# Lightning attention and snake MLP on one core: q in pieces of four tokens, freely placed PSUM banks, whole-row stores and a new instruction order

## The chip, the cores and the metric

The kernel runs on one core of a Trainium2 chip. The metric is the device time of one launch in microseconds (us). The kernel before takes 216.03 us, the median of 13 runs (214.77 to 218.7).

## What is computed

For each of 4 batches and 8 heads, a causal linear attention with decay runs over 768 tokens of 64 elements. Its output, 3072 tokens by 512, goes through an MLP (512 to 2048 to 512) with the "snake" activation.

```python
# attention, in blocks of 64 tokens, for each batch and head
intra = ((q_b @ k_b.T) * lam ** (i - j) for j <= i) @ v_b
inter = (q_b * lam ** (i + 1)) @ state
out_b = intra + inter
state = lam ** 64 * state + (k_b * lam ** (63 - j)).T @ v_b
# MLP on x = out as [3072, 512]
h = x @ w_in
g = h + sin(alpha * h) ** 2 / alpha
result = g @ w_out
```

## The kernel before

**Tiling.** The 3072 tokens are cut into 6 groups g of 512 tokens (256 tokens of each of two batches). A group has 4 attention units u (one batch, 4 heads, 256 tokens), so there are 24 units; units 8 and up add to the state that the unit 8 places before left. The MLP of a group is 16 first-layer tiles f1 (each 4 matmuls of 128x128 by 512 columns) and 4 output tiles m, each in 4 chunks f2.g.m.j of 4 such matmuls.

**Names in the order.** A unit runs through: `ld` (load of q, k, v, 256 KB each, SP queue, L259), `sq` and `sk` (scaling by powers of lam to bf16, L300), `cv` (cast of v), `tq`, `tk` (four TensorE transposes into PSUM, units 0 to 7, L327) with `tcq`, `tck` (copies back to SBUF), or `tdq`, `tdk` (transposing DMAs on SP, units 8 to 23, L345), `s` (16 score matmuls, L368), `m` (mask multiply on VectorE, two halves, L378), `k` (k times v, L400), `kc` (its copies), `a` (the new state, L425), `n` (the decayed state), `oi` (state times q, L446), `o` (masked scores times v, L460), and `x` (copy of the result to the MLP's input tile xt). The MLP has `f1` (`f1a` is the half of a tile that needs only a group's first two units), `sin` and `sqr` on the activations, `stt` (the final multiply-add on VectorE, L516), `f2` (L525), `oc` (copy of an output tile) and `st` (its store, L540). `lt` and `ltc` are the last tile, cut in three. `w.N` stands for N matmuls of zeros.

**What sets the order.** One string, ORDER, lists every step with its engine (V VectorE, A ScalarE, G GpSimd, T TensorE, S SyncE) and, for PSUM tiles, the bank. Each engine runs its steps in that order. Semaphores hold a step back until its data is there and its buffer or bank is free. So a late step holds back everything behind it on its engine.

**PSUM.** There are 8 banks, numbered 0 to 7. Before the change the two score halves always take banks 4 and 5 and the two outputs of a unit banks 6 and 7; transposes, k times v, f1 and f2 take the bank given in ORDER.

**Loads and stores.** A load puts token pairs on a partition: 128 partitions by 4 heads by 512 B. An output tile of 128 tokens is stored as two DMAs of 64 partitions by 2 KB, since even and odd tokens lie in different partition halves. Loads from unit 4 on are held until f1.0.12 has run. w_in and w_out come in four parts each on GpSimd's queue; the last part of w_out (`wo.3`) is issued by GpSimd after `a.0.1`.

**Tables.** GpSimd raises lam to the powers of the position in one instruction (L220); VectorE makes from it the table E for q and its reciprocal R for k, copies both to PSUM (`tab`), and then scales unit 0.

Of the kernel before, what the change touches and what calls it, by code (L numbers as in the profile page):

```python
# [9 lines left out]
ALU = mybir.AluOpType  # L10
# [8 lines left out]
tab:V ld.0.0:S sq.0:V ap:T w.4:T:h0 tq.0:T:0 ld.0.1:S ld.0.2:S sk.0:V cv.0:A w.3:T:h1 tk.0:T:5 al:V  # L19
tck.0:V ld.1.0:S ld.1.1:S ld.1.2:S ld.2.0:S ld.2.1:S ld.2.2:S ld.3.0:S tcq.0:A k.0:T:1,2 a.0.0:V  # L20
w.4:T:oa s.0:T sq.1:G sk.1:G sq.2:G kc.0.0:A kc.0.1:V m.0.0:V w.3:T:oa tq.1:T:2 w.3:T:oa tk.1:T:4
cv.1:A tcq.1:A k.1:T:0,1 oi.0:T m.0.1:V o.0:T x.0.0:A x.0.1:A tck.1:V kc.1.0:V kc.1.1:A a.1.0:V
s.1:T sk.2:V cv.2:A w.5:T:h2 tq.2:T:6 tk.2:T:1 w.2:T:h2 k.2:T:2,0 ld.3.1:S m.1.0:V m.1.1:V kc.2.0:V
kc.2.1:V wi.0:G wi.1:G a.2.0:V sq.3:G sk.3:G n.2.0:G wi.2:G n.0.0:G tcq.2:A w.1:T:ob oi.1:T tck.2:A
ld.3.2:S o.1:T x.1.0:A x.1.1:A cv.3:A s.2:T tq.3:T:1 w.4:T:oa oi.2:T tk.3:T:0 w.2:T:h2 k.3:T:2,3
m.2.0:V m.2.1:V o.2:T tck.3:V wi.3:G wo.0:G wo.1:G tcq.3:A s.3:T x.2.0:A a.3.0:V kc.3.0:V m.3.0:V
x.2.1:A m.3.1:V w.6:T:h1 oi.3:T f1a.0.0:T:0 f1a.0.1:T:4 o.3:T x.3.0:A kc.3.1:V f1a.0.2:T:3
f1a.0.3:T:2 wo.2:G x.3.1:V f1.0.0:T f1.0.1:T sin.0.0:A sin.0.1:A f1.0.2:T sqr.0.0:V stt.0.0:V
sqr.0.1:G stt.0.1:V f1.0.3:T f1.0.4:T:5 f1.0.5:T:7 sin.0.2:A sin.0.3:A sqr.0.2:A stt.0.2:V sqr.0.3:A
sin.0.4:A sqr.0.4:V sin.0.5:A f1.0.6:T:1 stt.0.3:V sin.0.6:A sqr.0.5:G f1.0.7:T:6 stt.0.4:V  # L30
f1.0.8:T:0 sqr.0.6:V stt.0.5:V stt.0.6:V f1.0.9:T:2 f1.0.10:T:4 f1.0.11:T:3 sin.0.7:A sin.0.8:A
sqr.0.7:G stt.0.7:V sqr.0.8:A stt.0.8:V n.1.0:G sin.0.9:A sqr.0.9:V a.1.1:G stt.0.9:V sin.0.10:A
sqr.0.10:G sin.0.11:A sqr.0.11:V f1.0.12:T:1 sin.0.12:A sqr.0.12:A a.0.1:G wo.3:G a.2.1:G n.2.1:G
stt.0.10:V stt.0.11:V f1.0.13:T:5 f1.0.14:T:7 sin.0.13:A sin.0.14:A n.0.1:G n.1.1:G n.3.0:G ld.4.0:S
ld.4.1:S ld.4.2:S ld.5.0:S ld.5.1:S ld.5.2:S ld.6.0:S sqr.0.13:V stt.0.12:V stt.0.13:V sqr.0.14:A
stt.0.14:V ld.6.1:S ld.6.2:S ld.7.0:S ld.7.1:S ld.7.2:S ld.8.0:S ld.8.1:S f2.0.0.0:T:0 f1.0.15:T:2
f2.0.0.1:T f2.0.1.0:T:6 sq.4:G f2.0.3.0:T:3 sin.0.15:A sqr.0.15:V f2.0.2.0:T:1 f2.0.1.1:T f2.0.2.1:T
stt.0.15:V f2.0.2.2:T f2.0.0.2:T f2.0.0.3:T f2.0.3.1:T oc.0.0:V a.3.1:G sk.4:G tq.4:T:7 tk.4:T:2
ld.8.2:S ld.9.0:S ld.9.1:S ld.9.2:S tck.4:V tcq.4:A f2.0.1.2:T s.4:T ld.10.0:S cv.4:A sq.5:G
tq.5:T:0 sk.5:G sq.6:G tcq.5:A f2.0.1.3:T oc.0.1:A sk.6:G tk.5:T:2 cv.5:G m.4.0:V f2.0.3.2:T m.4.1:V  # L40
k.4:T:6,7 a.4.0:V tck.5:A s.5:T m.5.0:V tq.6:T:0 cv.6:A tcq.6:V kc.4.0:A tk.6:T:2 m.5.1:V kc.4.1:A
ld.10.1:S ld.10.2:S f2.0.2.3:T tck.6:A oi.4:T k.5:T:0,2 o.4:T oc.0.2:A x.4.0:A x.4.1:A sq.7:G sk.7:G
s.6:T a.5.0:V kc.5.0:A kc.5.1:A f2.0.3.3:T tq.7:T:1 m.6.0:V m.6.1:V tcq.7:V cv.7:G n.3.1:G oi.5:T
oc.0.3:A sq.8:G tk.7:T:4 n.4.0:G sk.8:G tck.7:V a.4.1:G o.5:T k.6:T:0,2 k.7:T:1,3 x.5.0:A x.5.1:A
s.7:T n.5.0:G tdq.8:S a.6.0:V w.2:T:oa oi.6:T kc.6.0:A o.6:T a.7.0:V f1a.1.0:T:0 x.6.0:A m.7.0:V
n.4.1:G ld.11.0:S tdk.8:S ld.11.1:S x.6.1:A kc.6.1:V f1a.1.1:T:2 cv.8:A kc.7.0:A m.7.1:V oi.7:T
o.7:T k.8:T:4,5 f1a.1.2:T:1 x.7.0:V x.7.1:A f1.1.0:T f1.1.1:T f1.1.2:T kc.8.0:A sq.9:G f1a.1.3:T:4
f1.1.3:T kc.7.1:A f1.1.4:T:7 sin.1.0:A sin.1.1:A sin.1.2:A sk.9:G ld.11.2:S sqr.1.0:V stt.1.0:V
sin.1.3:A cv.9:A sqr.1.1:G stt.1.1:V sq.10:G sin.1.4:A sqr.1.2:V sqr.1.3:A stt.1.2:V stt.1.3:V
kc.8.1:V f1.1.5:T:3 sin.1.5:A f1.1.6:T:0 sqr.1.4:G sqr.1.5:G f1.1.7:T:6 f1.1.8:T:1 k.9:T:4,5  # L50
sin.1.6:A stt.1.4:V stt.1.5:V sin.1.7:A f1.1.9:T:2 kc.9.0:V sqr.1.6:A f1.1.10:T:7 kc.9.1:A sqr.1.7:A
tdq.9:S s.8:T a.8.0:G sk.10:G st.0.0.0:S ld.12.0:S tdk.9:S st.0.0.1:S stt.1.6:V stt.1.7:V sin.1.8:A
sqr.1.8:A sin.1.9:A sin.1.10:A stt.1.8:V m.8.0:V f1.1.11:T:3 f1.1.12:T:0 f1.1.13:T:1 sq.11:G
tdq.10:S sin.1.11:A f1.1.14:T:4 ld.12.1:S ld.12.2:S ld.13.0:S sqr.1.9:V sqr.1.10:A sqr.1.11:G
# [76 lines left out]
def kernel(  # L131
# [123 lines left out]
    def load(u, j, **_):  # L255
# [7 lines left out]
        if (u, j) == (4, 0):  # L263
            after(loads[u, j], f1mm[HOLD])
# [361 lines left out]
```

## Time and profile before

| what | value |
|---|---|
| median of 13 runs | 216.03 us |
| the profiled execution's own time | 216.56 us |
| its span, first to last instruction | 213.7 us |
| TensorE (PE) busy | 203.8 us, 95% |
| VectorE (DVE), ScalarE (ACT), GpSimd (POOL) busy | 129.9, 123.4, 141.5 us |
| mean granted TensorE clock | 0.998 |
| bytes moved by DMA | 33.92 MB in 64009 packets |

The page gives busy time by engine, the span in 40 slices, the chain of work that ended last, the costliest groups, and the DMA issues. PE's busy time is modelled, so the timeline's starts of successive groups tell more than the sums. A few matmul records are missing: where a group of 4n matmuls shows one fewer, the gap of about 0.16 us ahead of it is the missing record.

### The profile page before, as it was taken

How to read it: one execution, taken by the hardware profiler on the slowest of the kernel's cores; microseconds unless marked ns; L12 is line 12 of the kernel's file. 1: busy time of each engine (PE TensorE's matmuls, PEld its weight loads, DVE VectorE, ACT ScalarE, POOL GpSimd, SP SyncE). 2: the span in 40 equal slices, each digit the busy share in tenths (PEclk: the TensorE clock that was granted, in tenths of full speed). 3: DMA queues.
4: the chain of work that ended last, by engine and by line, in shares of the span. 5: the costliest groups of instructions: out<-in, count | busy, mean ns of one | idle time of the engine just before them, and what ended most of it. 6: DMA issues, size and time to landing. Idle time of an engine off the chain costs nothing.

```text
span 213.7 us, 5465 instructions
## 1 busy us (share of the span) xinstructions
PE 203.8 (95%) x2104; PEld 109.8 (51%) x2132; DVE 129.9 (61%) x235; ACT 123.4 (58%) x244; POOL 141.5 (66%) x208
## 2 busy tenths in 40 slices
PE   7989999899999979999999999999999999999993
PEld 6668544357744544455545554454454444444463
DVE  3885797159599843678768685726884625432120
ACT  3463983067899828997485496936635659131001
POOL 5498389689697997999999986709841728030000
PEclk9999999999999999999999999999999999999999
DMA  5999999999977999957997879620610000162624
GB/s 132 298 223 185 202 207 278 281 291 289 196 162 195 220 248 217 311 117 167 228 290 131 214 134 243 116 49 0 135 41 3 0 0 0 36 154 59 149 49 98
DMA packets 64009, 33.92 MB, mean 159 GB/s; under 512 B 19680, under 2 KB 61040, under 8 KB 63984
## 3 DMA queue, kind: packets, MB, share of 16 engines
q1 hardware_dynamic: 59568, 29.31, 60.3%
q0 software_dynamic: 4224, 4.19, 12.2%
q8 instruction: 16, 0.26, 0.6%
q10 hardware_dynamic: 192, 0.07, 0.2%
q14 instruction: 9, 0.07, 0.1%
HBM read 27.28 MB, written 6.29 MB: 157 GB/s over the span
## 4 chain that ended last, share of the span: by engine, by line
PE 72%; DMA 9%; POOL 5%; ACT 5%; issue 4%; SPq 2%; DVE 1%; POOLq 0%; ACTq 0%
PE ops L525 31%; PE hps L482 29%; DMA w_out_sb<-in_moe_w_out_dram 4%; ACT s L502 4%; PE okv L460 3%; DMA st_q<-in_q_dram 3%; DMA QT<-KD 2%; PE sp L368 2%; PE okv L446 2%; PE ops L550 2%; SPq L259 2%; POOL s L511 1%; PE kvp L400 1%; POOL QL L300 1%; POOL KD L300 1%
## 5 line engine op out<-in xcount | busy, mean ns | idle before, releaser
L482 PE MATMUL hps<-xt,w_in_sb 128*128 128x512 bf16 (+1 forms) x404 | 86.4, 363 | 0.6 <-issue 0.2
L525 PE MATMUL ops<-w_out_sb,gall 128*128 128x512 bf16 x352 | 83.2, 379 | 2.4 <-issue 1.3
L516 DVE SCALAR_TENSOR_TENSOR gall<-s,r_sb,hps 128x512 bf16<-128x512 bf16 x96 | 68.3, 743 | 23.8 <-POOL s L511 12.3
L502 ACT ACTIVATE s<-hps,alpha_sb 128x512 bf16<-128x512 f32 x96 | 63.2, 688 | 25.5 <-PE hps L482 24.6
L511 POOL TENSOR_TENSOR s<-s 128x512 bf16<-128x512 bf16 x35 | 36.3, 1045 | 37.3 <-ACT s L502 36.6
L482 PEld LDWEIGHTS <-w_in_sb 128*128 128x128 bf16 x416 | 39.7, 98 | 40.7
L525 PEld LDWEIGHTS <-gall 128*128 128x128 bf16 x368 | 34.6, 98 | 40.3 <-issue 1.0
L378 DVE TENSOR_TENSOR ST<-sp,mask 128x512 bf16<-128x512 f32 x48 | 31.8, 684 | 5.6 <-PE sp L368 5.4
L509 ACT ACTIVATE s<-s 128x512 bf16<-128x512 bf16 x51 | 31.6, 633 | 1.0 <-DVE gall L516 0.4
L300 POOL TENSOR_TENSOR QL<-st_q,E 128x512 bf16<-128x512 f32 x23 | 23.9, 1042 | 4.4 <-DVE r_sb L575 2.5
L284 DVE COPY ob<-ops 128x512 f32<-128x512 f32 (+1 forms) x13 | 8.6, 658 | 29.7 <-PE ops L525 23.4
L300 POOL TENSOR_TENSOR KD<-st_k,R 128x512 bf16<-128x512 f32 x22 | 22.9, 1042 | 1.9 <-DMA st_k<-in_k_dram 1.9
L425 POOL TENSOR_TENSOR kvbd<-kvx,LBD 128x256 bf16<-128x256 f32 x32 | 19.6, 612 | 2.5
L282 ACT COPY ob<-ops 128x512 f32<-128x512 f32 (+2 forms) x13 | 7.1, 546 | 22.9 <-PE ops L550 12.0
L282 ACT CAST xt<-okv 128x256 bf16<-128x256 f32 x29 | 9.8, 374 | 12.4 <-PE okv L460 12.4
L421 POOL TENSOR_TENSOR kvx<-kva,kvs 128x128 f32<-128x128 f32 x32 | 14.7, 460 | 0.8 <-ACT kva L282 0.6
L284 DVE CAST xt<-okv 128x256 bf16<-128x256 f32 x19 | 7.7, 420 | 9.6 <-PE okv L460 9.6
L282 ACT COPY kva<-kvp 128x128 f32<-128x128 f32 x26 | 6.4, 273 | 8.2 <-PE kvp L400 4.0
L368 PE MATMUL sp<-QT 64*64 64x128 bf16 x384 | 9.9, 220 | 1.0 <-DMA QT<-KD 1.0
L282 ACT COPY QT<-pt 128x512 bf16<-128x512 bf16 x9 | 5.2, 584 | 9.7 <-PE pt L327 9.7
L282 ACT CAST VB<-st_v 128x512 bf16<-128x512 f32 x14 | 8.6, 623 | 2.7 <-DMA st_v<-in_v_dram 2.7
L460 PE MATMUL okv<-ST,VB 64*64 64x128 bf16 x384 | 9.9, 220 | 0.0
(57 smaller groups left out, 126.2 us busy)
## 6 DMA issues: line engine op xcount, KB each, us to landing
st_q<-in_q_dram SPq DMA_DIRECT2D x24, 256.0 KB, 5.1
st_k<-in_k_dram SPq DMA_DIRECT2D x24, 256.0 KB, 5.4
st_v<-in_v_dram SPq DMA_DIRECT2D x24, 256.0 KB, 5.2
out_dram<-ob SPq DMA_DIRECT2D x46, 128.0 KB, 2.5
w_in_sb<-in_moe_w_in_dram POOLq DMA_DIRECT2D x4, 512.0 KB, 8.1
w_out_sb<-in_moe_w_out_dram POOLq DMA_DIRECT2D x4, 512.0 KB, 12.1
QT<-QL SPq DMA_TRANSPOSE x16, 3.3
QT<-KD SPq DMA_TRANSPOSE x16, 3.8
```

The lines of the kernel that those rows point to most:

```text
L282: nc.scalar.copy(out=out, in_=in_)
L284: eng.tensor_copy(out=out, in_=in_)
L300: eng.tensor_tensor(out=t[:], in0=stage[u, j][:].rearrange("p h two e -> p two h e"), in1=tab[:, :, hh * HH:(hh + 1) * HH].unsqueeze(3).to ...
L378: nc.vector.tensor_tensor(out=stm[u][:, hd], in0=sps[u][hd][:], in1=mask[:].unsqueeze(2).to_broadcast([P, 2, 2, P]), op=ALU.mult)
L425: eng.tensor_tensor(out=kvbd[u, c][:], in0=x.unsqueeze(2).to_broadcast([P, 2, 2, D]), in1=LBD[:, 2 * hh:2 * hh + 2, :].unsqueeze(3).to_bro ...
L460: nc.tensor.matmul(out=okv[u][c][half[hd], hp * P:(hp + 1) * P], lhsT=VB[half[c], par, 2 * hp + hd, :], rhs=ST[half[c], hd, par, hp, :], s ...
L482: f1mm[g, f] = nc.tensor.matmul(out=hps[g, f][:].rearrange("p (b i) -> p b i", b=2)[:, bs] .rearrange("p b i -> p (b i)"), lhsT=w_in_sb[:, ...
L502: nc.scalar.activation(out=s1[g, f][:], in_=hps[g, f][:], func=ACTF.Sin, scale=alpha_sb[:, f:f + 1])
L509: nc.scalar.activation(out=s2[g, f][:], in_=x[:], func=ACTF.Square)
L511: eng.tensor_tensor(out=s2[g, f][:], in0=x[:], in1=x[:], op=ALU.mult)
L516: nc.vector.scalar_tensor_tensor(out=gall[g][:, f, :], in0=s2.pop((g, f))[:], scalar=r_sb[:, f:f + 1], in1=hps.pop((g, f))[:], op0=ALU.mul ...
L525: nc.tensor.matmul(out=ops[g, m][:], lhsT=gall[g][:, f, m * P:(m + 1) * P], rhs=w_out_sb[:, f, :], start=(f == 0), stop=(f == NFC - 1))
```

## The change

Q is loaded four tokens to a partition: two DMAs per unit, one for each pair of heads, each to 64 partitions in 1 KB pieces. All that reads q follows: the table EQ (four powers, per partition half), the shape of QL and QT, and the right-hand operand of scores and state products, which is now four stretches of 32 columns in place of two of 64. The result of a unit comes out with the tokens in another order, and `x` writes it back in token order, so an output tile is 128 consecutive rows and one DMA stores it. Scores and unit outputs take the two banks that ORDER gives. ORDER is new from end to end; it has the same number of steps of every kind on TensorE (the zero matmuls too).

```diff
+    LQ = temp[:, 2 * P:2 * P + 4].rearrange("p (hh hd) -> p hh hd", hh=2)
...
+    lam_v = lam_bc[:].rearrange("p (hh hp hd) -> p hp hh hd", hh=2, hp=2)
+    for hp in range(2):
+        sl = slice(hp * D, (hp + 1) * D)
+        nc.vector.tensor_copy(out=LQ[sl], in_=lam_v[sl, hp])
+    nc.gpsimd.tensor_tensor(out=EQ[:, :, 0, :], in0=LQ,
+                            in1=posq.unsqueeze(2).to_broadcast([P, 2, 2]), op=ALU.pow)
     nc.gpsimd.tensor_tensor(out=E[:, 0], in0=lam_bc[:], in1=pos[:].to_broadcast([P, H]),
                             op=ALU.pow)
+    for i in range(3):
+        nc.vector.tensor_tensor(out=EQ[:, :, i + 1, :], in0=EQ[:, :, i, :], in1=LQ,
+                                op=ALU.mult)
     LT = consts.tile([P, H], FP32, name="LT")
...
+        if j == 0:
+            for hp in range(2):
+                loads[u, j] = nc.sync.dma_start(
+                    out=tl[hp * D:(hp + 1) * D].rearrange("p (hd i) two e -> p hd (i two e)", hd=2),
+                    in_=rows[2 * hp:2 * hp + 2].rearrange("hd (p t) e -> p hd (t e)", t=4))
...
-        sp = [ps.tile([P, 2, 2, P], FP32, name="sp", tag=f"s{hd}", bufs=1)
-              for hd in range(2)]
+        sp = [psum([P, 2, 2, P], FP32, "sp", i) for i in bank]
...
-                            rhs=QT[half[hd], 0, :, hp, half[c]],
+                            rhs=q_of(u, c, hp)[half[hd]],
...
-        okv[u] = [psum([P, 512], FP32, "okv", i) for i in (6, 7)]
+        okv[u] = [psum([P, 512], FP32, "okv", i) for i in bank]
...
-        copy(eng, xt[g][:, 2 * hh:2 * hh + 2, bb, c, :],
-             okv[u][c][:, 0:2 * P].rearrange("p (hp i) -> p hp i", hp=2))
+        copy(eng, xt[g][:, 2 * hh:2 * hh + 2, bb, c, :].rearrange(
+                 "p hp (i t) -> p hp t i", t=4),
+             okv[u][c][:, 0:2 * P].rearrange("p (hp t i) -> p hp t i", hp=2, t=4))
...
-    def store(g, m, par, **_):
-        nc.sync.dma_start(out=out_rows(g, m)[par], in_=obs[g, m][par * D:(par + 1) * D, :])
+    def store(g, m, _i, **_):
+        nc.sync.dma_start(out=out_rows(g, m), in_=obs[g, m][:])
```

Three stretches of the new ORDER, which the prediction speaks of (the string itself, cut). The units 4 to 7:

```
f2.0.1.2:T oc.0.0:V tck.4:V s.4:T:5,6 tq.5:T:2 f2.0.1.3:T tk.5:T:0 tcq.5:A oc.0.1:A f2.0.3.2:T
tq.6:T:3 tk.6:T:4 oc.0.2:V m.4.0:V m.4.1:V k.4:T:6,2 tck.5:A s.5:T:1,0 a.4.0:V f2.0.3.3:T tck.6:A
tcq.6:A kc.4.0:A kc.4.1:A oc.0.3:A k.5:T:5,3 tq.7:T:2 tcq.7:A m.5.0:V s.6:T:6,4 k.6:T:7,1 kc.6.0:A
kc.6.1:A m.5.1:V tk.7:T:0 a.5.0:V kc.5.0:V kc.5.1:V tck.7:A oi.4:T:5,2 o.4:T m.6.0:V m.6.1:V
oi.5:T:3,1 o.5:T a.6.0:V x.4.0:A x.4.1:A cv.7:G x.5.0:A s.7:T:6,0 w.2:T:h2 k.7:T:2,4 m.7.0:V
oi.6:T:7,3 ... cv.8:A a.7.0:V o.6:T x.5.1:A w.3:T:s1 f1a.1.0:T:5 m.7.1:V x.6.0:A oi.7:T:6,7 o.7:T
```

The same units before:

```
f2.0.3.2:T m.4.1:V k.4:T:6,7 a.4.0:V tck.5:A s.5:T m.5.0:V tq.6:T:0 cv.6:A tcq.6:V kc.4.0:A tk.6:T:2
m.5.1:V kc.4.1:A ... f2.0.2.3:T tck.6:A oi.4:T k.5:T:0,2 o.4:T oc.0.2:A x.4.0:A x.4.1:A ...
s.6:T a.5.0:V kc.5.0:A kc.5.1:A f2.0.3.3:T tq.7:T:1 m.6.0:V m.6.1:V tcq.7:V cv.7:G ... oi.5:T
oc.0.3:A ... tk.7:T:4 ... tck.7:V ... o.5:T k.6:T:0,2 k.7:T:1,3 x.5.0:A x.5.1:A s.7:T ... a.6.0:V
w.2:T:oa oi.6:T kc.6.0:A o.6:T a.7.0:V f1a.1.0:T:0 x.6.0:A m.7.0:V
```

Units 8 and 9, and units 16 to 19, after:

```
f2.1.0.0:T:0 f1.1.15:T:2 f2.1.0.1:T ... k.8:T:6,1 ... f2.1.0.2:T ... s.8:T:4,5 s.9:T:3,1 k.9:T:7,6
...
s.16:T:4,5 k.16:T:7 m.16.0:V m.16.1:V s.17:T:0,3 s.18:T:2,1 f2.2.3.1:T f2.2.3.2:T f2.2.3.3:T ...
oi.16:T:4,5 ... m.17.0:V m.17.1:V m.18.0:V m.18.1:V k.17:T:7 k.18:T:0 k.19:T:3 s.19:T:2,1
```

## The prediction

> **What bounds the kernel now.** I read the page's busy shares first, then PE's timeline, then the waits, then the chain that ended last.
>
> ```profile
> span 213.7 us, 5465 instructions
> PE 203.8 (95%) x2104; PEld 109.8 (51%) x2132; DVE 129.9 (61%) x235; ACT 123.4 (58%) x244; POOL 141.5 (66%) x208
> DMA  5999999999977999957997879620610000162624
> ```
>
> PE is the bound. DMA is busy in nine tenths of nearly every slice up to about 100 us, so a transfer can be late there. The timeline tells where PE really waits:
>
> ```profile
> 17.34 0.83 PE L588 MATMUL bz<-zeros 128*128 128x256 bf16 x6
> 18.00 0.28 PE L446 MATMUL okv<-QT,kvbd 128*128 128x128 bf16 x2
> 18.11 1.04 PE L482 MATMUL hps<-xt,w_in_sb 128*128 128x256 bf16 x8
> ...
> 41.06 1.89 PE L525 MATMUL ops<-w_out_sb,gall 128*128 128x512 bf16 x8 [0.71 <-DMA w_out_sb<-in_moe_w_out_dram]
> ...
> 76.24 0.42 PE L368 MATMUL sp<-QT 64*64 64x128 bf16 x16 [1.02 <-DMA QT<-KD]
> ```
>
> The MLP starts at 18.11. From there to PE's end at 210.1 these are the only two idle stretches that count: 0.71 us on the last part of w_out, 1.02 us on unit 8's transposed k. The other marked waits, 0.16 us "issue" each, stand before groups that show one matmul too few, so they are missing records. The chain of waits gives DMA 9%, but most of that passes beside a busy PE. So the most that this change can take from PE after 18.11 is about 1.8 us; PE's own steps stay the same in number. What else can change is the 18 us ahead, and new waits.
>
> **Part 1, the tables at the start: +0.8 us.** Unit 0 waits for the tables:
>
> ```profile
> 3.77 0.17 DVE L224 TENSOR_TENSOR LT<-lam_bc 128x8 f32<-128x8 f32 x1 [1.69 <-DMA lam_bc<-in_lam_dram]
> 3.82 1.67 POOL L220 TENSOR_TENSOR E<-lam_bc,pos 128x8 f32<-128x8 f32 x1 [1.27 <-DMA lam_bc<-in_lam_dram]
> 3.97 1.17 DVE L226 TENSOR_TENSOR LT<-LT 128x8 f32<-128x8 f32 x6
> 5.53 0.17 DVE L227 TENSOR_TENSOR E<-E,lam_bc 128x8 f32<-128x8 f32 x1 [0.39 <-POOL E L220]
> ...
> 6.31 0.69 DVE L300 TENSOR_TENSOR QL<-st_q,tab 128x512 bf16<-128x512 f32 x1
> ```
>
> lam is there at 3.77. After the change DVE first makes LQ (two small copies, about 0.16 each, from the table copy at 5.90), to 4.1. Then POOL raises EQ to its powers, 128x4; the trace has no such row. Its bounds are a small POOL instruction (IOTA, 0.13) and E itself (1.67, twice the elements). I take 0.9, about half of E: to 5.05. POOL's E follows, to 6.7. On DVE three EQ products (0.17 each) and the seven LT steps (1.34) stand between: to 6.95. From E's second half to `sq.0` took 6.31 - 5.53 = 0.78, so `sq.0` starts at about 7.7, 1.4 later (0.8 to 2.2 at the bounds).
>
> Not all of it reaches the MLP. DVE works through the same list in both orders, from `sq.0` to `m.3`, 6.31 to 18.82, and it stands idle for only about 1.0 us of that (0.14 before `sk.2`, 0.30 before `m.2`, 0.42 before `tck.3`, 0.17 before `a.3.0`). Those idles hang on loads and on POOL's `sk.3`, which the tables hardly move, since POOL's `sq.1` began only at 7.97. Most of them now absorb the delay: 1.4 - 0.6 = +0.8. I leave 0.4 standing because `tk.3` now comes behind `oi.2` and five zero matmuls on PE. Bounds +0.2 to +1.6. PE idles 1.8 us before `tq.0` (0.38 before), with nothing else to do. From 19 on PE is busy, so the delay is carried to the end.
>
> **Part 2, q in two DMAs of 1 KB pieces: 0.** The trace's loads are 512 B packets at a mean of 31.8 ns (64 ns per KB). The nearest row of longer pieces from 64 partitions is the stores: 2 KB packets at 136.7 ns, 68 ns per KB. By these the pieces gain nothing and lose little: a q load is a third of the traffic, 6% of it is 2%, on 10 us of loads at the start 0.2 us. The other bound is the w_in transfers: about 98 ns per packet of 2 KB read, 49 ns per KB, which would bring the last loads of the start 0.7 us sooner; DVE's late start would hide most of that. SP issues 24 more loads and 23 fewer stores at 0.4 to 0.8 us each. In the built program each DMA waits for the one 8 places before it, so 6 tiles are in flight in place of 8; at some 290 GB/s and 5 us to landing that still fills the engines.
>
> [...]
>
> **Part 3, units 4 to 7: +1.1 us.** Before, f2.0 chunks lie between these units' steps up to 50.41, and `o.7` ends at 54.17: 3.76 us in which PE has 2.98 of work (`tq.7`, `tk.7` 0.21 each; `k` 0.2, `s` and `o` 0.25, `oi` 0.1 each; f1a 0.43). 0.78 is lost. The new order spends its last f2.0 chunk just after `s.5`. Count from that chunk's end, T. PE has 3.35 of work left up to `o.7` and nothing to fill with. DVE's list is `a.4.0`, `m.5` (twice), `a.5.0`, `kc.5` (twice), `m.6` (twice), `a.6.0`, `m.7.0`, `a.7.0`, `m.7.1`. Its steps followed each other like this before:
>
> ```profile
> 49.65 1.29 DVE L378 TENSOR_TENSOR ST<-sp,mask 128x512 bf16<-128x512 f32 x2
> 50.86 0.74 DVE L284 COPY QT<-pt 128x512 bf16<-128x512 bf16 x2
> 51.70 0.75 DVE L425 TENSOR_TENSOR kvbd<-kvp,LBD 128x256 bf16<-128x256 f32 x2
> ```
>
> With 0.64 for `m`, 0.37 for `a` and 0.25 for `kc` the list takes 6 x 0.64 + 4 x 0.37 + 2 x 0.25 = 5.8 us. It can't start before `k.4` is done, and that lies one `s.5` and one f2 chunk ahead of T: T - 1.0. So `m.7.1` ends at T + 4.85 and `o.7` at about T + 5.2. ACT is as tight: `tck.6`, `tcq.6`, `kc.4` twice, `oc.0.3`, `tcq.7`, `kc.6` twice, `tck.7` (0.53 or 0.25 each) let `s.7` go at T + 2.6, where PE would be at T + 2.1. Lost: 5.2 - 3.35 = 1.85, against 0.78: +1.1. Bounds 0 (the extra idle is made up by f2 work done earlier) and +2.2 (waits for banks of `okv` added).
>
> **Part 4, waits that go: -1.4 us.** Unit 8's `s` now stands behind f1.1.15 and two f2.1 chunks, some 7 us of PE work later, while POOL's `sk.8` stays where it was: the 1.02 goes, whole. At the w_out wait, `tq.4` (0.21) is now put ahead, and two tiles fewer are queued ahead of it: of 0.71 I take 0.4 off (0 to 0.7). Next late in both places is DVE, and it has room there.
>
> **Part 5, new bank waits: +0.5 us.** `s.19` takes banks 2 and 1, which `s.18` held, so it needs `m.18.1`: six mask halves after `s.16`, 3.9 us. PE gets there after `k.16`, `s.17`, `s.18`, three f2 chunks, `oi.16`, three `k`: 3.65. That is 0.3, and 0.2 more for units 9 to 11, where `oi.9` and `k.11` take banks that `m.10` frees. For units 12 to 15 and 20 to 23, DVE's masks (5.2 us for eight halves) fit under the f2 chunks between (over 5 us of PE work in 8 us).
>
> **Part 6, at nothing.** Matmuls that read four stretches of 32 columns stream as many columns: 0, or at the worst twice the time of the scores, 20 x 0.22 = +4.4. `x` writing every fourth element: 0.37 us on ACT and 0.42 on DVE with slack after; if each grew by half, some 0.2 us would show in each of five groups, +1.0. The single store instead of two: stores end in PE's shadow but for the last, whose two 32 KB halves landed in 1.9 to 2.0 us; 0, or 0.2 either way. Changes of PE between quarter-array and whole-array work: 52 to 50, -0.2 at most; I take 0.
>
> **Sum.** +0.8 + 0 + 1.1 - 1.4 + 0.5 = +1.0 us. The profiled execution took 216.56 us (213.7 span and 2.9 around it), so 217.6 by it; its time is 0.5 over the median of the runs, 216.03, so **217.0 us**.
>
> **Rivals.**
> *Free banks pay (faster), 0.20.* The two idle stretches go and part 3's hole closes: it decides where `m.7.1` ends by T + 3.9 (then no more is lost than before), for instance if `m.5` runs under the last f2 chunk. Then +0.4 - 1.7 + 0.2 = -1.1: 214.9, and 214.6 if loads are sooner as well. For: PE's idle and these banks. Against: DVE's list, 5.8 us long.
> *They cancel, 0.20.* Part 3 costs 0.3 and the start 0.6: 0 to within 0.6, 215.4 to 216.6. Differences under 0.3% can't be told from no change here.
> *The start costs all of it, 0.10.* If POOL's second power takes the full 1.67, and halves of a load run at the pace of a whole one (0.9 us each, four in the start), `sk.3` becomes the late one and the MLP starts 3 us late: 219.5. For: both bounds. Against: 68 ns per KB in the stores.
> *The forecast, 0.50*, own range 216.7 to 218.6.
>
> Slower: 0.50 + 0.10 = 0.60; same 0.20; faster 0.20. The range takes in the fast rival's end and the start's: 214.6 to 219.6.
>
> **What would show it.** Right: `sq.0` at 7.5 to 8.0; first f1 matmul at about 18.9; 1.5 to 2 us of PE idle or zero matmuls in the units 4 to 7; no wait on QT at unit 8. Wrong: an MLP start at 18.1 or sooner, score groups longer than 0.35, st_q halves landing after 6 us, or PE idle past 80 us.

## The result and the profile after

The changed kernel takes **220.62 us**, the median of 11 runs (219.59 to 222.92), and the kernel before, beside it, 216.59 us (48 runs). The ratio is 1.0224, with a 95% interval of 1.0191 to 1.0257. So it is 4.0 us slower; the forecast was 1.0 slower, and the time lies above the range. The direction was right and the size wrong.

The profiled execution took 223.24 us; the clock fell in two of its slices (6 in the row PEclk, from 56 to 66 us, treated further down), and it is longer than the median. So times are compared by the other executions, and its timeline is read mainly ahead of that fall. From its page:

```profile
span 221.2 us, 5456 instructions
PE 208.9 (94%) x2106; PEld 111.6 (50%) x2132; DVE 132.1 (60%) x235; ACT 137.2 (62%) x251; POOL 140.9 (64%) x211
PEclk9999999999669999999999999999999999999999
DMA  4999999999997589999669983139550000023132
GB/s 123 253 247 190 201 208 218 250 213 212 257 223 178 102 251 246 238 287 171 155 162 198 261 206 71 27 77 116 144 164 4 3 0 0 0 74 118 47 144 95
```

Read the last line against the same line of the kernel before:

```profile
GB/s 132 298 223 185 202 207 278 281 291 289 196 162 195 220 248 217 311 117 167 228 290 131 214 134 243 116 49 0 135 41 3 0 0 0 36 154 59 149 49 98
```

Its slices 7 to 10 (32 to 53 us) have 278, 281, 291 and 289 GB/s. After the change these slices (33 to 55 us) have 218, 250, 213 and 212, though the bytes asked for are the same. The DMA engines are busy for nine tenths of each of these slices, as before, and move less. GpSimd waits 9.6 us in all for loads of q, before 1.0. ScalarE is busy for 137.2 us, before for 123.4. TensorE's timeline up to the second group:

```profile
18.77 0.72 PE L623 MATMUL bz<-zeros 128*128 128x256 bf16 x5
19.55 1.03 PE L518 MATMUL hps<-xt,w_in_sb 128*128 128x256 bf16 x8
...
42.73 1.89 PE L561 MATMUL ops<-w_out_sb,gall 128*128 128x512 bf16 x8 [0.72 <-DMA w_out_sb<-in_moe_w_out_dram]
...
55.32 0.38 PE L403 MATMUL sp<-QT 64*64 64x128 bf16 x13 [1.49 <-issue]
...
58.59 0.59 PE L518 MATMUL hps<-xt,w_in_sb 128*128 128x256 bf16 x2 [0.55 <-ACT xt L305]
```

The MLP starts 1.44 us later than before. The wait on w_out is still there. In units 4 to 7 TensorE stands for 1.49 us (the profile names no releaser) and for 0.55 on a copy `x`. The wait of 1.02 us on a transposing DMA, which the prediction puts at unit 8, is gone.

ScalarE's own timeline tells what held that copy:

```profile
53.27 1.87 ACT L305 CAST xt<-okv 128x256 bf16<-128x256 f32 x3
57.29 0.62 ACT L305 CAST VB<-st_v 128x512 bf16<-128x512 f32 x1 [2.15 <-DMA st_v<-in_v_dram]
57.82 1.29 ACT L305 CAST xt<-okv 128x256 bf16<-128x256 f32 x2
```

`cv.8` waits 2.15 us for its load of v, and the copies of `x` queued behind it wait too. V is loaded just as before; it is late all the same. That was the first sign that the loads of q slow the other loads.

### The profile page after: what moved, and what is told of

Same layout as the page of the kernel before. It is cut to its first block, busy times and chain, and to the rows that moved or that the text cites. A ratio compares the mean times of both kernels' runs of the same rounds, so it can differ in the third digit from the quotient of the medians.

```text
span 221.2 us, 5456 instructions
## 1 busy us (share of the span) xinstructions
PE 208.9 (94%) x2106; PEld 111.6 (50%) x2132; DVE 132.1 (60%) x235; ACT 137.2 (62%) x251; POOL 140.9 (64%) x211
## 4 chain that ended last, share of the span: by engine, by line
PE 74%; DMA 10%; SPq 4%; ACT 3%; issue 3%; POOL 2%; DVE 2%; POOLq 0%; ACTq 0%
PE hps L518 33%; PE ops L561 31%; DMA w_out_sb<-in_moe_w_out_dram 4%; DMA st_v<-in_v_dram 4%; PE okv L495 2%; DMA st_q<-in_q_dram 2%; PE sp L403 2%; SPq L279 2%; PE okv L481 2%; PE ops L586 2%; ACT s L538 2%; SPq L285 1%; PE kvp L435 1%; ACT xt L305 1%; DVE gall L552 1%
## 5 line engine op out<-in xcount | busy, mean ns | idle before, releaser
L518 PE MATMUL hps<-xt,w_in_sb 128*128 128x512 bf16 (+1 forms) x406 | 89.1, 371 | 1.4 <-ACT xt L305 0.7
L518 PEld LDWEIGHTS <-w_in_sb 128*128 128x128 bf16 x416 | 41.2, 100 | 44.9 <-issue 2.5
L547 POOL TENSOR_TENSOR s<-s 128x512 bf16<-128x512 bf16 x32 | 33.3, 1046 | 26.3 <-ACT s L538 25.3
L413 DVE TENSOR_TENSOR ST<-sp,mask 128x512 bf16<-128x512 f32 x48 | 30.8, 686 | 5.1 <-PE sp L403 5.0
L324 POOL TENSOR_TENSOR QL<-st_q,EQ 128x512 bf16<-128x512 f32 x23 | 23.9, 1042 | 12.0 <-DMA st_q<-in_q_dram 9.6
L305 ACT CAST xt<-okv 128x256 bf16<-128x256 f32 x31 | 20.6, 777 | 9.4 <-PE okv L495 9.0
L305 ACT COPY ob<-ops 128x512 f32<-128x512 f32 (+2 forms) x16 | 8.9, 558 | 25.6 <-PE ops L561 21.0
L307 DVE COPY ob<-ops 128x512 f32<-128x512 f32 (+1 forms) x10 | 6.5, 649 | 26.6 <-PE ops L561 18.9
L307 DVE CAST xt<-okv 128x256 bf16<-128x256 f32 x17 | 11.5, 745 | 8.8 <-PE okv L495 8.7
L305 ACT COPY QT<-pt 128x512 bf16<-128x512 bf16 x12 | 6.8, 588 | 9.0 <-PE pt L366 8.9
```

The lines of the kernel that those rows point to most:

```text
L305: nc.scalar.copy(out=out, in_=in_)
L307: eng.tensor_copy(out=out, in_=in_)
L324: eng.tensor_tensor(out=t[:], in0=stage[u, 0][:].rearrange("p (hd i) two e -> p (i two) hd e", hd=2), in1=tab[:, hh].unsqueeze(3).to_broad ...
L413: nc.vector.tensor_tensor(out=stm[u][:, hd], in0=sps[u][hd][:], in1=mask[:].unsqueeze(2).to_broadcast([P, 2, 2, P]), op=ALU.mult)
L518: f1mm[g, f] = nc.tensor.matmul(out=hps[g, f][:].rearrange("p (b i) -> p b i", b=2)[:, bs] .rearrange("p b i -> p (b i)"), lhsT=w_in_sb[:, ...
L547: eng.tensor_tensor(out=s2[g, f][:], in0=x[:], in1=x[:], op=ALU.mult)
```

## The experiments

**Theories.** *D*: the two 64-partition loads of q carry less than one 128-partition load and hold up all that shares the queue. *O*: the order costs it, by units 4 to 7 and bank waits, as the prediction had it. *X*: the result copies `x`, which write every fourth element. *T*, added later: the tables at the start.

Two numbers of each trace tell more than the time: the SP queue's rate, which is the bytes of its packets that start from about 41.4 to 51.4 us into the span, over 10 us (the expectations call this stretch 40 to 50 us); and the start of the first multiply-add of group 0 and of group 1 on VectorE's timeline.

| kernel | median us | ratio to before, same chip | KB/us, 41.4 to 51.4 | group 0 | group 1 |
|---|---|---|---|---|---|
| before | 216.59 | 1 | 288 | 22.21 | 56.75 |
| e1 change again | 219.97 | 1.016 (1.0074 to 1.0247) | 243 | 23.60 | 61.13 |
| e2 order only | 215.58 | 0.9983 (0.9944 to 1.0023) | 290 | 21.84 | 57.77 |
| e3 layout only | 223.18 | 1.0304 (1.0213 to 1.0394) | 233 | 24.29 | 63.53 |
| e4 q in one load | 217.12 | 1.0059 (1.0022 to 1.0097) | 290 | 23.33 | 59.79 |
| *plain copies for the transposing DMAs:* | | | | | |
| g1 before | 214.18 | 0.9932 (0.9896 to 0.9968) | 288 | 22.20 | 56.77 |
| g2 after | 218.69 | 1.0155 (1.0111 to 1.0198) | 236 | 23.66 | 61.31 |
| g3 g1, q in halves | 217.92 | 1.015 (1.0085 to 1.0214) | 241 | 24.28 | 59.52 |
| g4 g2, q wide 1 KB | 217.41 | 1.0111 (1.008 to 1.0143) | 313 | 23.50 | 61.04 |
| g5 g2, x contiguous | 217.96 | 1.0041 (0.9999 to 1.0083) | 245 | 23.62 | 62.57 |
| g6 g2, early table | 219.0 | 1.0095 (1.0052 to 1.0137) | 254 | 23.29 | 60.28 |
| g7 g2, all three out | 213.6 | 0.9867 (0.9808 to 0.9927) | 290 | 22.20 | 57.73 |
| g8 g1, new order | 215.29 | 0.9952 (0.9924 to 0.998) | 282 | 22.22 | 57.86 |
| h1 g1, q by heads | 215.1 | 0.9976 (0.9932 to 1.0019) | 282 | 22.21 | 56.60 |
| h2 g1, q and k in halves | 226.95 | 1.0518 (1.0424 to 1.0613) | 245 | 25.13 | 60.41 |
| h3 g2 again | 218.6 | 1.0091 (1.005 to 1.0131) | 262 | 23.59 | 60.70 |
| h4 h3, q in one load | 216.54 | 1.0016 (0.998 to 1.0052) | 291 | 23.32 | 59.17 |

Each ratio is to the kernel before on the same chip; its medians there lie between 215.71 and 216.59. A ratio isn't the quotient of the two medians: g3 is 1.7% above g1 by the medians and 2.2% by the ratios. So less than about 1 us is not to be leaned on. The profiles of e1, e3 and g5 took 224.02, 224.37 and 219.39 us, above their medians, so their last columns are less sure than the rest.

The rate depends on the window. From 40.0 to 50.0 us of the span, g4 has 295 in place of 313, h1 292 in place of 282, g1 292 and g3 231. In both windows every kernel with halves lies between 216 and 262 and every other between 282 and 313; differences inside either set tell nothing.

### The change taken apart: e1 to e4

e1 is the changed kernel unaltered.

> The changed kernel once more, unaltered, for a profile at the full clock: in the first one two of the 40 slices ran at 0.6 of it. Median 220 to 221. Theory D (the half-partition q loads slow the transfers): in the stretch 40 to 60 us the profile again moves about 210 to 250 GB/s where the kernel before moves 280 to 290, and the idle of TensorE is again between 52 and 60 us. Theory O (the new order alone, as forecast): the idle there is there, but the loads are long landed. Theory X (the result copies, which now write every fourth element and take 0.75 us in place of 0.4): waits of TensorE on xt or on ScalarE and VectorE in all groups, not only in the second.

e2 is the kernel before with the new ORDER, the free banks, and both half stores of a tile at the place of the single one:

```diff
-        sp = [ps.tile([P, 2, 2, P], FP32, name="sp", tag=f"s{hd}", bufs=1)
-              for hd in range(2)]
+        sp = [psum([P, 2, 2, P], FP32, "sp", i) for i in bank]
-        okv[u] = [psum([P, 512], FP32, "okv", i) for i in (6, 7)]
+        okv[u] = [psum([P, 512], FP32, "okv", i) for i in bank]
```

> The kernel before with the new order and the free PSUM banks, but the old q layout: one load of 128 partitions, contiguous result copies, the old tables, two stores per row tile. Theory O: the loss is the order's, so 219 to 221. Theories D and X: 215.5 to 217.5, since both causes are taken away with the layout.

e3 is the changed kernel with the old ORDER and the fixed banks; its single store stands where the first half store stood.

> The changed kernel with the old order (scores in banks 4 and 5, outputs in 6 and 7; each row tile stored once, at the place of its first half's store). Theory O: only the tables' delay is left, 217 to 218. Theories D and X: 219.5 to 223, since layout, loads and strided copies are all kept and the order was not made for them.

e4 is the changed kernel with q's load as before, so the pieces of q that it computes with are other tokens:

```diff
-            for hp in range(2):
-                loads[u, j] = nc.sync.dma_start(
-                    out=tl[hp * D:(hp + 1) * D].rearrange("p (hd i) two e -> p hd (i two e)", hd=2),
-                    in_=rows[2 * hp:2 * hp + 2].rearrange("hd (p t) e -> p hd (t e)", t=4))
+        loads[u, j] = nc.sync.dma_start(
+            out=tl[:].rearrange("p h two e -> p h (two e)"),
+            in_=rows.rearrange("h (p two) e -> p h (two e)", two=2))
```

> The changed kernel with q loaded as before in one DMA of 128 partitions by 4 pieces of 512 B; tokens of q then lie in the wrong places, so the numbers are not the reference's, but every step is there. Theory D: the transfer rate returns to 280 to 290 GB/s in 40 to 50 us, unit 8's v lands some 4 us sooner, and the time falls to 217.5 to 219. Theory X: within 0.5 of the changed kernel. Theory O: within 0.5 of the changed kernel.

By the medians (before 215.86 beside them): order -0.28 (e2), tables, copies and the rest of the layout +1.54 (e4 less e2), q's halves +2.85 (e1 less e4); together 4.11, which is e1 less before. By the ratios, in the same order: -0.4, +1.6 and +2.2 us. Theory O falls: e2 can't be told from before. The halves are the largest part, and the rate falls with them, from 290 to 243 KB/us. e4 came out a little below what theory D said, 217.5 to 219.

The parts don't simply add. e3, the layout under the old order, is 3.2 us above e1 (1.0304 against 1.016). So the new order is worth some 3 us under the new layout and nothing measurable under the old one. In e3's profile TensorE waits 2.31 us for w_out and 1.08 and 0.91 us for transposing DMAs.

The split also hides a gain at the end. From TensorE's last matmul to the end of the span it is 3.5 us before, 4.2 in e2 and g8, where the two half stores of a tile follow each other, and 3.1 in every kernel with single stores. So e4's +1.54 over e2 holds about 1.1 us won by the stores. By TensorE's end, 210.13 before, 209.41 in e2 and 211.35 in e4, the order wins 0.7 us, and tables and copies cost 1.9.

The order does cost something in units 4 to 7: e2 is 0.37 us ahead at group 0 and 1.02 us behind at group 1. Later it wins that back; its span, 213.6, is that of before.

### Is it the halves? g1 to g4

The other kernels have a plain DMA in the place of each transposing one, so that the attention of units 8 to 23 isn't computed and no wait on a transposing DMA mixes in; all up to unit 8 stays. The edit, for both layouts:

```diff
-        nc.sync.dma_start_transpose(
-            out=qkt[u][:, j], in_=blocks(u, j).rearrange("p i m -> p (i m)"))
+        nc.sync.dma_start(
+            out=qkt[u][:, j].rearrange("p i m -> p (i m)"),
+            in_=blocks(u, j).rearrange("p i m -> p (i m)"))
```

> The base of a second family. The kernel before with each of its 32 transposing DMAs replaced by a plain DMA of the same bytes, at the same place of the same queue; the attention of units 8 to 23 is then not computed, and only the time is read. What lies ahead of unit 8 (the start, the loads of units 0 to 12, units 0 to 7) is untouched. All theories: 213.5 to 216.5 us, that is the kernel before or a little less, since a plain copy should land sooner than the 3.3 and 3.8 us of the transposing ones; 40 to 50 us into the span the SP queue moves 280 to 295 KB/us.

> The changed kernel with the same replacement of its 32 transposing DMAs, so that the attention of units 8 to 23 isn't computed. If what the change costs lies in the loads, the tables and the copies x (theories D and X), it is as far above g1 as the changed kernel above the kernel before, 3 to 5 us, and the rate 40 to 50 us into the span is 215 to 250 KB/us. If what it costs lies in the transposing DMAs behind unit 8 (the wait of 4.14 us on one that e1 shows), it is less than 2 us above g1.

g3 is the kernel before with nothing altered but q's load, still in 512 B pieces:

```diff
-        loads[u, j] = nc.sync.dma_start(
-            out=tl[:].rearrange("p h two e -> p h (two e)"),
+        for i in range(2 if j == 0 else 1):
+            n = P // 2 if j == 0 else P
+            loads[u, j] = nc.sync.dma_start(
+                out=tl[i * n:(i + 1) * n].rearrange("p h two e -> p h (two e)"),
...
```

> g1 with one thing altered: each q load is two DMAs of 64 partitions, still in 512 B pieces; nothing else of the change is in it (and the attention of units 8 to 23 isn't computed). Theory D (two loads to partition halves carry less than one load to 128 partitions, and slow all that shares the queue): the rate 40 to 50 us into the span is 215 to 250 KB/us instead of 288, a 512 B packet takes 37 to 46 ns instead of 33, and the time is 2 to 5 us above g1. Rival P (the 1 KB pieces are what is slow, not the halves): 280 to 295 KB/us, and within 1 us of g1.

g4 is g2 with q as one DMA of 128 partitions by two 1 KB pieces:

```diff
-            for hp in range(2):
-                loads[u, j] = nc.sync.dma_start(
-                    out=tl[hp * D:(hp + 1) * D].rearrange("p (hd i) two e -> p hd (i two e)", hd=2),
-                    in_=rows[2 * hp:2 * hp + 2].rearrange("hd (p t) e -> p hd (t e)", t=4))
+            t0 = min(tp * W, 256)
+            loads[u, j] = nc.sync.dma_start(
+                out=tl[:].rearrange("p (hd i) two e -> p hd (i two e)", hd=2),
+                in_=src[b, hh * HH:hh * HH + 2, t0:t0 + 512, :]
+                .rearrange("hd (p t) e -> p hd (t e)", t=4))
```

> g2 with each q load as one DMA of 128 partitions by two 1 KB pieces, taken from two heads and 512 tokens in place of four heads and 256; so it computes with other tokens of q, and the attention of units 8 to 23 isn't computed. Theory D: the rate 40 to 50 us into the span is 280 KB/us or more, and the time 0.5 to 1.5 us above g1. Rival P: 215 to 250 KB/us, and the time that of g2. Third case, that 1 KB pieces carry more than 512 B pieces when they go to 128 partitions: over 300 KB/us, and a time within 0.5 us of g1 or below it.

g3 costs 3.7 us over g1 (4.7 by the ratios) and brings the rate down as far as the whole change does. The pieces are not at fault: in g4 the 1 KB pieces go to 128 partitions and the rate is no lower than with 512 B pieces (313 against 288, and 295 against 292 in the window 1.4 us sooner). The mean time of a 1 KB packet in the table's window is 54 ns there and 78 ns in g2; the 512 B packets of k and v take 31.5 in g4, 41.9 in g2.

Two thirds of what g3 loses is lost ahead of the MLP. TensorE waits there 1.7 us in all for casts of v (one wait is in the first line; before it was 0.2), and the MLP starts at 20.18 us, in g1 at 18.10:

```profile
15.36 0.32 PE L402 MATMUL kvp<-VB,KD 64*64 64x64 bf16 x16 [0.77 <-ACT VB L284]
...
20.18 1.04 PE L484 MATMUL hps<-xt,w_in_sb 128*128 128x256 bf16 x8
```

By group 1 it is 2.75 us behind, and at TensorE's end 3.1.

A miss is g4's time: 217.41, 3.2 us above g1 where 0.5 to 1.5 was expected by theory D. It has the tables, the copies and the order of g2; h4, which has them too, is 2.4 above g1. At TensorE's end g4's profile is 0.96 us behind h4's: 0.2 at the start of the MLP, and 0.61 on w_out that h4 hasn't. (At group 1 it is 1.9 behind; most of that is made up by group 2.)

### 64 partitions, or two DMAs? h1 to h4

h1 splits q's load by heads, so there are two DMAs of 128 KB as in g3, but each goes to all partitions; h2 is g3 with k in halves too.

```diff
+        n = HH // 2 if j == 0 else HH
+        for h0 in range(0, HH, n):
+            loads[u, j] = nc.sync.dma_start(
+                out=tl[:, h0:h0 + n].rearrange("p h two e -> p h (two e)"),
...
```

> The control to g3: g1 (the kernel before with plain copies for its transposing DMAs; the attention of units 8 to 23 isn't computed) with each q load as two DMAs of two heads each, so two DMAs of 128 KB as in g3, but each to all 128 partitions. Theory D (64 partitions carry less): 40 to 50 us into the span 280 to 295 KB/us, as in g1, and the time within 0.5 us of g1, 213.7 to 215.2. Rival N (the number of DMAs is what costs, their issue on the SP queue and a fixed time for each): 235 to 255 KB/us and 217 to 219 us, as in g3.

> The suspected cost doubled: g3 with k too in two DMAs of 64 partitions (the attention of units 8 to 23 isn't computed). Theory D: if a third of the bytes in halves takes the rate 40 to 50 us into the span from 288 to 241 KB/us, two thirds take it to 200 to 215, and the time to 220 to 224 us. If the halves only cost a fixed pause where the queue passes from one kind to the other, the rate stays at 230 to 245 and the time within 1 us of g3's 217.9.

> g2 a second time, for a comparison with h4, g5 and g6 on other chips' terms (the attention of units 8 to 23 isn't computed): 218 to 219.5 us, a ratio of 1.010 to 1.018 to the kernel before.

> h3 with q loaded as in the kernel before, one DMA of 128 partitions in 512 B pieces, so that it computes with other tokens of q (and the attention of units 8 to 23 isn't computed). Theory D as sized by e1 and e4 (1.016 and 1.006): 1.5 to 3 us below h3. If the halves cost only where transposing DMAs follow: within 0.5 us of h3.

The rows of moved bytes on the pages of g1, g3, and h1, one fence each:

```profile
GB/s 129 299 215 206 204 203 275 283 287 292 295 219 204 185 292 309 214 148 112 306 243 244 126 216 27 75 49 0 171 6 3 0 0 0 42 170 38 150 49 99
```

```profile
GB/s 101 245 243 197 185 207 242 246 232 250 252 216 223 267 235 220 282 215 198 185 233 208 253 216 74 100 49 0 140 37 3 0 0 0 24 173 49 146 49 97
```

```profile
GB/s 134 298 227 172 197 206 272 270 289 259 260 242 275 193 231 275 260 198 125 255 263 206 199 150 81 72 49 0 149 30 3 0 0 0 42 172 36 148 49 99
```

Slices 1 and 2 are the start: 129 and 299 GB/s with one load, 101 and 245 with two halves, 134 and 298 with two DMAs by heads. So it is the 64 partitions; a second DMA by itself costs nothing that these runs can tell (h1 0.9976, g1 0.9932, with intervals that overlap). Nor is it that six tiles are in flight in place of eight, since h1 has as many DMAs per tile as g3.

h2 costs more again: 3.7 us for q's halves, 12.8 for q's and k's (226.95 less 214.18), above the 220 to 224 us expected. Its runs spread from 222.68 to 232.2, and its profile, of the 222.68, has a wait of 2.68 us on a copy of k and a fall of the clock, so 12.8 is not the load's price alone. At the start the rate falls further with the dose, 223 KB/us from 3.4 to 13.4 us where g3 has 241 and g1 294. In the table's window it is 245, not the 200 to 215 expected, so the loss there isn't in proportion to the bytes in halves.

h3 and h4, timed together, give the halves' share in the changed kernel without transposing DMAs: 218.6 - 216.54 = 2.1 us, or 0.75% by the ratios, which is 1.6 us.

### Copies and tables: g5 to g8

g5 writes `x` side by side, so that the rows of each tile of 128 come out in another order:

```diff
-        copy(eng, xt[g][:, 2 * hh:2 * hh + 2, bb, c, :].rearrange(
-                 "p hp (i t) -> p hp t i", t=4),
-             okv[u][c][:, 0:2 * P].rearrange("p (hp t i) -> p hp t i", hp=2, t=4))
+        copy(eng, xt[g][:, 2 * hh:2 * hh + 2, bb, c, :],
+             okv[u][c][:, 0:2 * P].rearrange("p (hp i) -> p hp i", hp=2))
```

> g2 (the changed kernel with plain copies for its transposing DMAs; the attention of units 8 to 23 isn't computed) with the result copies x written side by side and not to every fourth element, so that the rows of each tile of 128 come out in another order. Theory X (the doubled copies, 777 ns for 374 on ScalarE and 745 for 420 on VectorE, hold the path ahead of the second group): the wait of 0.66 us of the first-layer matmuls on ScalarE's copy of xt at 56.4 us goes, and the time is 0.4 to 1.0 us below g2's 218.69, 217.7 to 218.3. If the copies lie beside other work: within 0.3 us of g2.

The groups of these copies, in the changed kernel and then in g5 (busy time, mean ns, idle before):

```profile
L305 ACT CAST xt<-okv 128x256 bf16<-128x256 f32 x31 | 20.6, 777 | 9.4 <-PE okv L495 9.0
L307 DVE CAST xt<-okv 128x256 bf16<-128x256 f32 x17 | 11.5, 745 | 8.8 <-PE okv L495 8.7
```

```profile
L305 ACT CAST xt<-okv 128x256 bf16<-128x256 f32 x31 | 10.4, 382 | 11.8 <-PE okv L496 11.7
L307 DVE CAST xt<-okv 128x256 bf16<-128x256 f32 x17 | 6.7, 421 | 8.4 <-PE okv L496 7.8
```

The strided write costs ScalarE 395 ns a copy and VectorE 324. Where it reaches TensorE is to be seen in e4, whose queue is fast, so that no late load mixes in:

```profile
53.22 0.38 PE L617 MATMUL bz<-zeros 128*128 128x256 bf16 x2 [0.67 <-ACT xt L299]
```

g5 hasn't that wait (it has one of 1.85 us on w_out); its time is 0.6 us below h3, with intervals that overlap (0.9999 to 1.0083 and 1.005 to 1.0131). About half a microsecond is likely; the run doesn't settle it.

g6 copies q's table and scales unit 0's q ahead of the work on k's table:

```diff
-ld.0.0:S ld.0.1:S ld.0.2:S tab:V ap:T cv.0:A sq.0:V w.4:T:h0
+ld.0.0:S ld.0.1:S ld.0.2:S tab:V ap:T cv.0:A sq.0:V tak:V w.4:T:h0
... (both lines cut here)
...
+    def table_k(eng, **_):
+        nc.vector.tensor_tensor(out=E[:, 1], in0=E[:, 0], in1=lam_bc[:], op=ALU.mult)
+        nc.vector.reciprocal(out=R[:], in_=E)
+        copy(eng, tabs[0][:, 1], R[:].rearrange("p two h -> p (two h)"))
```

> g2 with q's table copied and q of unit 0 scaled ahead of the work on k's table, and the six squarings of lam put into the wait for q's powers (the attention of units 8 to 23 isn't computed). Theory T (the start costs what the tables add on VectorE): the first scaling of q starts at 6.0 to 6.3 us instead of 7.55, the first f1 at 18.7 to 19.1 instead of 19.55, and the time is 0.5 to 1.0 us below g2's 218.69. Rival (the start then waits for the loads, which the halves slow): the first f1 at 19.3 or later, and the time within 0.3 us of g2.

g7 has the edits of h4, g5 and g6 together. g8 is e2 with plain copies.

> g2 with the three suspects taken out together: q loaded as before (one DMA of 128 partitions in 512 B pieces, so other tokens of q), the early table of g6 and the contiguous x of g5; the attention of units 8 to 23 isn't computed. If loads, tables and copies are all that the layout costs, it comes within 0.5 us of g8, near 214. If something else of the layout costs (the right-hand operand of four stretches, the single stores), it stays over 1 us above g8.

> g1 (the kernel before with plain copies for its transposing DMAs; the attention of units 8 to 23 isn't computed) with the new order and the free banks of the change, two stores per tile at one place, and nothing of the new layout. The steps on record for the order: units 4 to 7 come out later (first multiply-add of the second group at 57.5 to 58 us instead of 56.8, as in e2), and nothing is won back behind it, since the wait on a transposing DMA at unit 8 isn't there in g1: 0.5 to 1.2 us above g1, 214.6 to 215.4. If the order is as good as the old one also without that wait: within 0.3 us of g1.

The first scaling of q on VectorE, and TensorE's first f1 group, in g6 and then in g7:

```profile
5.93 0.69 DVE L326 TENSOR_TENSOR QL<-st_q,tab 128x512 bf16<-128x512 f32 x1
```

```profile
19.20 1.03 PE L521 MATMUL hps<-xt,w_in_sb 128*128 128x256 bf16 x8
```

```profile
6.21 0.69 DVE L320 TENSOR_TENSOR QL<-st_q,tab 128x512 bf16<-128x512 f32 x1
```

```profile
18.09 1.05 PE L514 MATMUL hps<-xt,w_in_sb 128*128 128x256 bf16 x8
```

In g6 `sq.0` is 1.6 us sooner than in the changed kernel and the MLP starts only 0.35 sooner; GpSimd then waits 3.6 us for the loads of q. With the loads repaired as well, in g7, the whole 1.4 us is there, and 18.09 is the start of before. With the loads alone repaired, in e4, it starts at 19.24. So the start has two chains of nearly the same length, tables and loads, and taking out one shows next to nothing.

g7 reaches 213.6 us (0.9867). So the halves, the tables and the copies are all that the layout costs; four stretches for the scores' operand and single stores cost nothing. It is even below g8 (215.29, 0.9952), 1.7 us by the medians with intervals that overlap barely. In the two profiles g7 is 1.2 us shorter, and 1.1 of it lies behind TensorE's last matmul, in the stores. g8 came out as expected for the order.

No version that computes the reference beats both kernels here: e2 is the best, and not to be told from before. g7's load of q reads other tokens. In the layout a partition is a pair of heads and four tokens, two strides in memory, and q comes in two loads of one stride each; a layout with one stride was not tried.

## Why the prediction failed, point by point

**Part 2 is the step that failed**: "q in two DMAs of 1 KB pieces: 0", with -0.7 as the other bound. It measured +2.85 us (e1 less e4), +2.1 (h3 less h4) and +3.7 in the old order (g3 less g1); by the ratios +2.2, +1.6 and +4.7. I priced a packet by "64 ns per KB" and "68 ns per KB in the stores" and took the likeness of the two for safety. But the stores were themselves 64 partitions wide. Their 2 KB packets take 137 ns on the mean before, and 89 ns after the change, with 128 partitions. So the nearest row held the loss, and the row to set beside it, the w_in transfers at 49 ns per KB, stood in the same paragraph as a gain. The medians of e1 to e4 lie 3.1 us over the forecast of 1.0; 2.85 of that is this step, 0.7 is tables and copies beyond the 0.8 of part 1, and the order took 0.5 less than parts 3 to 5 said. The page's rows of issues fit that, before and after (KB each, median us to landing):

```profile
st_q<-in_q_dram SPq DMA_DIRECT2D x24, 256.0 KB, 5.1
...
out_dram<-ob SPq DMA_DIRECT2D x46, 128.0 KB, 2.5
```

```profile
st_q<-in_q_dram SPq DMA_DIRECT2D x48, 128.0 KB, 5.0
...
out_dram<-ob SPq DMA_DIRECT2D x23, 256.0 KB, 2.7
```

A half store lands hardly sooner than a whole one, and a half load of q no sooner than a whole one did. These rows alone prove little: in h1, where two DMAs by heads cost nothing, the halves land in 4.4 us, in g3 in 4.5.

I also asked only for the price of q's own bytes. What the halves did was to slow k and v beside them (512 B packets 32.8 ns in g1, 39.9 in g3). Unit 8's cast `cv.8` starts at 57.29 us in the change's profile, at 55.39, 55.12 and 54.28 in e1, g2 and h3, and at 53.45 in e4 and h4, where q is one load. Which wait of TensorE shows the loss differs from profile to profile: the copies behind `cv.8` in the change's own, 1.51 us on w_out in e1, the start of the MLP in g3.

g1, g3 and h1 give the loss its size: the queue moved 288 KB/us with q in one load, 241 with two loads to 64 partitions each, a sixth less, and 282 with two loads to 128. Why loads to 64 partitions carry less, no run here shows.

**Part 1, the tables (+0.8).** The working held: EQ's powers took 1.04 us (0.9 taken), `sq.0` started at 7.55 (7.7). The MLP started 1.44 later, within the bounds. In GpSimd's and VectorE's timelines of the changed kernel:

```profile
3.94 1.04 POOL L232 TENSOR_TENSOR EQ<-ob 128x4 f32<-128x4 f32 x1 [0.60 <-DVE ob L231]
```

```profile
5.02 0.56 DVE L237 TENSOR_TENSOR EQ<-EQ,ob 128x4 f32<-128x4 f32 x3 [1.16 <-POOL EQ L232]
...
7.55 0.69 DVE L324 TENSOR_TENSOR QL<-st_q,tab 128x512 bf16<-128x512 f32 x1
```

So `sq.0` came 1.24 us late. The assumption that idle stretches absorb 0.6 of the delay was wrong: even e4, with the loads as before, starts the MLP 1.13 late (19.24).

**Part 3, units 4 to 7 (+1.1).** Right in kind, a little small: from the end of the last f2.0 chunk to the end of `o.7` both e2 and g8 need 5.5 us (5.2 forecast), the kernel before 3.8; TensorE's work there is 3.35 and 2.98, so 1.4 more is lost. The multiply-adds show it too: e2 falls back 1.4 us from group 0 to group 1, and g8, without any transposing DMA, 1.1 (57.86 against 56.77).

**Part 4, waits that go (-1.4).** The 1.02 went, in e2 and in the changed kernel, but not for the reason given. It didn't stand at unit 8: in the kernel before the score groups at 63.54, 71.12, 73.26 and 76.24 us are those of units 8 to 11, and the last of them waited. Its transposing DMA is issued at 70.9 us before and at 67.1 in e2, with the scores at 75.6. That unit 8's scores come later has no part in this, so the size was right by luck. The w_out wait went only in part of the runs. It is 0.72 in the changed kernel, 1.51 in e1, 1.85 in g5, 0.61 in g4 and 0.42 in e2, and nothing in the seven other profiles of the new order, with halves (g2, h3, g6) or without (e4, g7, g8, h4). What decides it these runs don't show.

**Part 5, bank waits (+0.5).** The only new idle stretch past 80 us in the changed kernel that could be one is 0.36 at 87.25, without a named releaser; at `s.19`, where 0.3 was forecast, there is none. So bank waits aren't shown. Parts 3 to 5 together were to be +0.2; e2 measures -0.28 with an interval of about 0.8 on both sides, and -0.7 by TensorE's end.

**Part 6, at nothing.** Matmuls of four stretches: right, the score matmuls take 219 ns on the mean against 220. Stores: a little better than the 0.2 allowed, 3.1 us behind the last matmul in place of 3.5. The copies `x` were said to grow by half and to cost 1.0 then, and I took none of it; they doubled, and cost about 0.5.

**The rivals.** "Halves of a load run at the pace of a whole one" named the cause and gave 219.5, nearest to the result (3 us at the start with the forecast's other terms, +0.2, make 219.2). In the changed kernel it failed in its place: it put the whole cost into the start, where the halves add only 0.3 to what the tables cost (19.24 in e4, 19.51 in e1), and nothing behind 20 us. In g3, where the tables are the old ones, its place was right for 2.1 us: the start has two chains, and the table chain of the change covers most of what the loads lose there. My sign against it, halves that land after 6 us, was set too high, at more than a whole load takes (5.1 us at the median).

**What stays open.** In the changed kernel the halves cost 2.85 us, without transposing DMAs 2.1 (2.2 and 1.6 by the ratios). One execution of e1 shows what could make the rest, a transposing DMA that is late at unit 12:

```profile
105.62 0.64 PE L403 MATMUL sp<-QT 64*64 64x128 bf16 x16 [4.14 <-DMA QT<-KD]
```

The profile of the change hasn't that wait, and the intervals of both figures are wider than the 0.75 us between them, so this isn't shown.

## What to carry to other kernels

Ask of a load first how many partitions it goes to, and only then how long its pieces are: two loads to 64 partitions slowed the loads beside them (512 B packets 39.9 ns in g3, 32.8 in g1), while two loads to 128 showed no cost (h1 215.1 us, g1 214.18, with intervals that overlap). When a trace has no row for a transfer, look for the same bytes in half and in whole width, and price the neighbours that share the queue, not the transfer alone. And where two chains meet at one point, undo both: either alone showed a quarter or less of what the two were worth (0.35 us in g6 and 0.3 in e4, of 1.4 in g7).

## What the runs showed of the hardware that was not expected

**The wider stores were faster as well.** A store's 2 KB packet takes 137 ns on the mean where a DMA takes from 64 partitions (before; 134 in e2), and 88.9 where it takes from 128 (after; 88.5 in e4).

**A strided 2-byte write about doubled a copy.** 374 to 777 ns on ScalarE, 420 to 745 on VectorE, for 128x256 from PSUM with every fourth element written; 382 and 421 with the elements side by side (g5).

**The clock was halved after a short hole.** In the profiled execution of the change TensorE did 0.68 us of work from 54 to 56 us. These are that stretch and those from 58 us on (width, then TensorE's busy time; the granted clock stands behind the engines):

```profile
54.00:56.00 2.00, 0.68 (x15) 0.33 (x14) 0.27 (x1) 1.14 (x3) 0.00 (x0) 1.00 1.22 211
...
58.00:60.00 2.00, 1.45 (x21) 0.76 (x19) 0.00 (x0) 1.84 (x4) 1.48 (x3) 0.50 1.16 272
60.00:62.00 2.00, 2.00 (x14) 1.42 (x11) 0.73 (x1) 0.73 (x1) 1.91 (x3) 0.50 1.01 333
62.00:64.00 2.00, 2.00 (x11) 1.45 (x10) 0.42 (x1) 0.96 (x2) 1.32 (x2) 0.50 1.07 240
...
66.00:68.00 2.00, 2.00 (x11) 0.93 (x10) 1.70 (x4) 2.00 (x4) 0.78 (x2) 1.00 0.74 143
```

The clock was 0.85 from 56 to 58 us and 0.94 from 64 to 66. So it was halved for over six microseconds, which is some 3 us lost, about what this execution took above the median. The longest single wait before the fall was 1.49 us, with little work around it. In h2 a wait of 2.68 us was followed by 0.50 from 84 to 86 us. That the hole brought the clock down is read from the order of time; no run tried it. Most executions of the change kept their clock at 1.0 and were still slower than before, so this is no part of the 4.0 us.
